# Retention and mixture of adapters, end of the program: two of six stores by Pool's queue, and one copy out of PSUM on ScalarE instead of VectorE

## The chip, the cores and the metric

The kernel runs on one core of a Trainium2 chip. The time is the device time of one execution in microseconds (us); the number that counts is the median over several runs. Beside it a profile of one further execution is there. Its span is the time from the first to the last instruction of the program on the core's engines, and the device time of that execution is a little longer than its span.

## The reference

Queries, keys and values have 8 batches, 8 heads, 576 positions and 64 columns, all in float32. First retention is computed: scaled scores, damped by a power of a constant of the head for each position of distance, nothing from the future, and then times the values. The heads are put side by side, which gives 4608 rows of 512. Each row then picks 2 of 8 adapters.

```
gamma = 1.0 - 2.0 ** (-5.0 - np.arange(H))
Dmat  = np.where(rel >= 0, gamma ** rel, 0.0)
attn  = np.matmul(scale * np.matmul(q, kT) * Dmat, v)
x     = attn.transpose(0, 2, 1, 3).reshape(B * S, H * D)
topk  = two largest of x @ w_gate, w = softmax over these two
out   = x + sum over the two: w * (x @ A[e]) @ B[e]
```

## The kernel before

The work is cut into units. A full unit is a chunk of 128 positions for two batches; a half unit is the last 64 positions (512 to 575) for four batches. For each four batches there are eight full units and one half unit, so `NU` is 18. The very last unit, `END`, is a half unit, and `END - 1` is the full unit before it. The order of the work is written out by hand: each engine does its instructions in the order in which the code emits them, and an instruction waits only for the data that it needs. A loop over the units keeps TensorE busy with the products of one unit while VectorE, ScalarE and Pool prepare operands for the next ones and copy results out of PSUM.

What matters here is what follows the loop, from L1028 on. The adapters of the last unit are chosen in two halves, n = 0 and n = 1, so that the second half can begin while the first is under way. After that the results leave PSUM in three steps:

- `osn_out(nc.vector, END - 1, n)`, for n = 0 and 1: VectorE copies half n of unit `END - 1` from the PSUM tile `po` to the SBUF tile `osb`, as 128 partitions by 512 values.
- `osh_out(END, 0, o, nc.scalar)`, for o = 0 and 1: ScalarE copies half 0 of unit `END`, in two pieces of 128 by 256, one for each of two PSUM banks.
- `osh_out(END, 1, o, nc.vector)`, for o = 0 and 1: VectorE copies half 1 of unit `END` in the same way. `Yn_mm` at L655 writes the two banks one after the other.

Then six stores are issued:

- `store(END - 1)` gives two stores (L702) of 128 rows of 2 KB, which is 256 KB each, one for each n. Both are issued by SyncE (SP in the profile).
- `store_rows(END, n, (nc.sync, nc.scalar))` gives, for each n, two stores (L717) of 64 rows of 2 KB, 128 KB each: `par` = 0 takes the lower 64 partitions and is issued by SyncE, `par` = 1 takes the upper 64 and is issued by ScalarE.

An engine that issues a store first waits until the copy has filled that part of `osb`. The stores of one engine are issued in the order of the code. At the end of the program (L1102) SyncE waits for all stores to land, after which the engines meet once more and the program is over. Pool (`nc.gpsimd`) issues two loads in the whole kernel before: `Wg` at L737 (16 KB) and `Bcat` at L903 (128 KB, with a conversion from float32 to float16). Pool's last computation is `q_turn` of the last unit, long before the end.

Of the kernel before, what the change touches and what calls it, by code (L numbers as in the profile page):

```python
# [21 lines left out]
def kernel(  # L22
# [10 lines left out]
    nc = tc.nc  # L33
# [91 lines left out]
    def full(u):  # L125
        return units[u][0] < NFULL
# [54 lines left out]
    def copy(eng, out, in_):  # L181
        if eng is nc.scalar:
            nc.scalar.copy(out=out, in_=in_)  # L183
        else:
            eng.tensor_copy(out=out, in_=in_)  # L185
# [489 lines left out]
    def osh_out(u, n, o, eng):  # L675

        s = st[u]
        copy(
            eng, s["osb"][:, n, :].rearrange("p (a o d) -> p o a d", a=HP, o=2)[:, o],
            s["pn"][n][o],  # L680
        )
# [6 lines left out]
            s["po"][:, :, n],  # L688
        )

    def store(u):
        c, bp = units[u]
        of = st[u]["osb"]
        tok = out.rearrange("(b s) d -> s b d", s=S)
        if full(u):


            parts = [(0, 0, 119), (1, 0, 128), (0, 119, 128)]
            if u > NU - 4:
                parts = [(0, 0, 128), (1, 0, 128)]  # L700
            for n, lo, hi in parts:
                nc.sync.dma_start(  # L702
                    out=tok[128 * c + lo : 128 * c + hi, 2 * bp + n, :], in_=of[lo:hi, n, :]
                )
            return
        for par in range(2):
            b = 4 * bp + 2 * par
            nc.sync.dma_start(
                out=tok[128 * c : 128 * c + 64, b : b + 2, :], in_=of[HALF[par]]
            )  # L710

    def store_rows(u, n, eng):

        c, bp = units[u]
        tok = out.rearrange("(b s) d -> b s d", s=S)
        for par in range(2):
            eng[par].dma_start(  # L717
                out=tok[4 * bp + 2 * par + n, 128 * c : 128 * c + 64, :],
                in_=st[u]["osb"][HALF[par], n, :],
            )  # L720
# [215 lines left out]
    osb_open(0)  # L936
    osb_out(nc.scalar, 0)
    store(0)
    route_s(1)
    U_out(2)  # L940
# [24 lines left out]
    END = NU - 1  # L965
    for r in range(2, END):
# [39 lines left out]
        osb_open(r - 1)  # L1006
        osb_out(nc.vector if nn < NU else nc.scalar, r - 1)
        store(r - 1)
        if nn < NU:
            T_open(nn, "q", "S")  # L1010
# [58 lines left out]
    for o in range(2):  # L1069
        osh_out(END, 0, o, nc.scalar)  # L1070
    for o in range(2):
        osh_out(END, 1, o, nc.vector)
    store(END - 1)
    for n in range(2):
        store_rows(END, n, (nc.sync, nc.scalar))
    return


# [28 lines left out]
```

## Time and profile before

| what | value |
|---|---|
| median of 3 runs | 180.52 us (180.03 to 184.05) |
| the profiled execution, device time | 180.89 us |
| the profiled execution, span | 179.1 us |
| mean granted TensorE clock | 0.991 of full speed |
| TensorE (PE) busy | 172.0 us, 96% of the span |
| VectorE (DVE) busy | 131.3 us, 73% |
| Pool busy | 121.9 us, 68% |
| ScalarE (ACT) busy | 77.5 us, 43% |

So the profiled execution lies 1.8 us above its own span, and 0.37 us above the median of the runs. In rows of the profile, PE, DVE, ACT, POOL and SP are the engines, and a name with a q behind it (SPq, ACTq) is that engine's instruction queue, where DMAs are issued and waited for. The DMA queues have numbers: q1 carries what SyncE issues, q10 what ScalarE issues, and q0, called software_dynamic, what Pool issues. Times of a timeline are us from the start of the span, start first, duration second.

### The profile page before, as it was taken

Reading aid. Unit: us, or ns where it says so; the run is one execution under the profiler, and the core shown is the slowest. Engines: PE = TensorE matmul, PEld = TensorE weight load, DVE = VectorE, ACT = ScalarE, POOL = GpSimd, SP = SyncE. Lnnn points to the kernel's source line nnn. Section 1 sums busy time; section 2 is a strip of 40 time slices with the busy share of each in tenths; the row PEclk is TensorE's granted clock in tenths of the full one; section 3 lists DMA queues with packets and bytes.
Section 4 is the critical chain, followed back from the end, with each engine's and each line's share of the span. In section 5 each row is a group of like instructions: output and inputs, shape, how many; then the busy total and the mean of one; then the engine's idle time right before and its main releaser. Section 6 shows DMA issues by size and latency. Waiting matters only on the chain.

```text
span 179.1 us, 9384 instructions
## 1 busy us (share of the span) xinstructions
PE 172.0 (96%) x4126; PEld 156.7 (87%) x4126; DVE 131.3 (73%) x236; ACT 77.5 (43%) x158; POOL 121.9 (68%) x208
## 2 busy tenths in 40 slices
PE   7999999999999999999999999999999999999990
PEld 5799988989999999989989999999998999889960
DVE  6586475789696968687676686969696869687870
ACT  0743644925252535352726362625252444443330
POOL 7990676497888688787994929585868677792000
PEclk9999999999999999999999999999999999999996
DMA  4999999989898989998999998999999999974125
GB/s 116 280 261 247 256 207 203 232 201 216 208 262 201 262 197 253 222 224 200 266 223 252 230 268 193 239 223 239 231 249 205 252 217 249 213 205 152 48 105 202
DMA packets 119368, 39.00 MB, mean 218 GB/s; under 512 B 114320, under 2 KB 114720, under 8 KB 119328
## 3 DMA queue, kind: packets, MB, share of 16 engines
q1 hardware_dynamic: 113360, 36.51, 84.1%
q10 hardware_dynamic: 5792, 1.75, 4.1%
q8 instruction: 32, 0.52, 1.1%
q0 software_dynamic: 176, 0.15, 0.5%
q14 instruction: 8, 0.07, 0.1%
HBM read 29.09 MB, written 9.44 MB: 215 GB/s over the span
## 4 chain that ended last, share of the span: by engine, by line
PE 95%; DVE 2%; issue 1%; DVEq 0%
PE pz L487 20%; PE px L432 18%; PE pu L395 9%; PE ps L322 9%; PE pt_k L248 6%; PE px L451 6%; PE po L620 5%; PE pt_q L248 5%; PE ps L304 4%; PE po L605 4%; PE pf L728 3%; PE pzt L587 2%; DVE M L373 2%; PE pa L514 1%; PE ps L338 1%
## 5 line engine op out<-in xcount | busy, mean ns | idle before, releaser
L373 DVE TENSOR_TENSOR M<-ps,tri 64x1024 f32<-64x1024 f32 (+1 forms) x34 | 37.3, 1097 | 4.8 <-PE ps L322 4.0
L185 POOL COPY M<-Qs 64x512 f32<-64x512 f32 x34 | 20.8, 612 | 26.1 <-ACT Qs L183 25.3
L487 PE MATMUL pz<-AW,xT 128*128 128x136 f32 x288 | 37.7, 284 | 0.0
L432 PE MATMUL px<-M,W 128*64 128x128 f32 (+1 forms) x640 | 35.4, 263 | 0.4 <-DVE M L373 0.4
L487 PEld LDWEIGHTS pz<-AW,xT 128*128 128x128 f32 x288 | 34.6, 190 | 0.6
L226 POOL TENSOR_TENSOR k<-k,pack 128x1024 f32<-128x1024 f32 (+1 forms) x18 | 32.5, 1808 | 2.4 <-POOL V L185 0.8
L185 POOL COPY W<-v 64x256 f32<-64x256 f32 x78 | 28.9, 396 | 7.5 <-DMA v<-in_v_dram 5.8
L183 ACT COPY kT<-pt_k 128x1024 f32<-128x1024 f32 x17 | 17.3, 1016 | 37.6 <-PE pt_k L248 37.6
L432 PEld LDWEIGHTS px<-M,W 128*64 128x64 f32 x640 | 31.8, 137 | 0.8 <-POOL k L226 0.6
L470 DVE TENSOR_TENSOR xT<-px,gx 128x1024 f32<-128x1024 f32 x11 | 13.5, 1225 | 15.7 <-PE px L451 14.1
L185 DVE COPY osb<-po 128x1024 f32<-128x1024 f32 (+2 forms) x18 | 19.2, 1074 | 6.0 <-PE po L620 5.3
L596 ACT COPY zT<-pzt 128x256 f16<-128x256 f16 (+1 forms) x19 | 6.9, 362 | 36.6 <-PE pzt L587 36.6
L183 ACT COPY M<-pt_q 64x512 f32<-64x512 f32 x35 | 20.2, 577 | 1.1 <-PE pt_q L248 0.6
L395 PE MATMUL pu<-v,k 128*64 128x64 f32 x512 | 18.4, 225 | 0.0
L322 PE MATMUL ps<-Qs,kT 64*64 64x128 f32 (+1 forms) x304 | 18.2, 260 | 0.0
L322 PE MATMUL ps<-M,kT 64*64 64x128 f32 (+1 forms) x304 | 18.0, 259 | 0.0
L188 POOL TENSOR_TENSOR W<-pn,W 64x512 f32<-64x512 f32 x12 | 15.3, 1273 | 3.7 <-ACT pn L183 2.9
L395 PEld LDWEIGHTS pu<-v,k 128*64 128x64 f32 x512 | 16.2, 138 | 1.1
L322 PEld LDWEIGHTS ps<-M,kT 64*64 64x64 f32 x304 | 14.9, 134 | 0.2
L322 PEld LDWEIGHTS ps<-Qs,kT 64*64 64x64 f32 x304 | 14.9, 134 | 0.0
L248 PEld LDWEIGHTS pt_k<-ident,k 64*128 64x128 f32 x272 | 9.9, 139 | 3.2 <-issue 2.9
L185 POOL COPY V<-v 64x256 f32<-64x256 f32 x32 | 12.0, 401 | 0.7
(75 smaller groups left out, 298.8 us busy)
## 6 DMA issues: line engine op xcount, KB each, us to landing
v<-in_v_dram SPq DMA_DIRECT2D x36, 256.0 KB
q<-in_q_dram SPq DMA_DIRECT2D x35, 256.0 KB
k<-in_k_dram SPq DMA_DIRECT2D x33, 256.0 KB
out_dram<-osb SPq DMA_DIRECT2D x20, 256.0 KB
out_dram<-osb SPq DMA_DIRECT2D x14, 238.0 KB
k<-in_k_dram ACTq DMA_DIRECT2D x3, 256.0 KB
An<-in_moe_A_dram ACTq DMA_DIRECT2D x1, 256.0 KB
q<-in_q_dram ACTq DMA_DIRECT2D x1, 256.0 KB
```

Of the source, the lines that this page charges most:

```text
L183: nc.scalar.copy(out=out, in_=in_)
L185: eng.tensor_copy(out=out, in_=in_)
L188: eng.tensor_tensor(out=out, in0=a, in1=b, op=ALU.add)
L226: eng.tensor_tensor(out=kt, in0=kt, in1=gv[:, c, :].unsqueeze(1).unsqueeze(3).broadcast_to((128, bs.stop - bs.start, H, Dh)), op=ALU.mult,)
L248: mm(ps[:, r, hp, b, :], lhsT=src[HALF[r], b * H + 2 * hp : b * H + 2 * hp + 2, :], rhs=ident[HALF[r], 64 * r : 64 * r + 64], is_transpose ...
L322: mm(s["ps0"][HALF[1 - p], b, hp, sl], lhsT=s["kT"][HALF[ho], x, hp, b, :], rhs=Q_of(u, b, ho, hp, sl), start=(hp == 0 and x == 0), stop=True,
L373: nc.vector.tensor_tensor(out=s["M"][sl, p, bs].rearrange("p b a i -> p (b a) i"), in0=s["ps0"][sl, bs].rearrange("p b a i -> p (b a) i"), ...
L395: mm(s["pu"][HALF[p], b, hp, :], lhsT=nat[("k", u)][:, h, :], rhs=nat[("v", u)][:, h, :], start=(hp == 0 and b == 0), stop=True, skip_grou ...
L432: mm(s["pxb"][b][HALF[ho], hp, sl], lhsT=s["W"][x][:, p, b, hp, :], rhs=s["M"][:, p, b, hp, sl], start=(hp == 0 and x == 0), stop=True, sk ...
L451: mm(s["px"][HALF[ho], b, hp, HI], lhsT=vv, rhs=s["S1"][HALF[p], b, hp, :], start=False, stop=True, skip_group_check=True,)
L470: nc.vector.tensor_tensor(out=s["xT"][:, bs].rearrange("p b a i -> p b (a i)"), in0=s["px"][:, bs].rearrange("p b a i -> p b (a i)"), in1= ...
L487: mm(s["pz"][:, n, :], lhsT=s["xT"][:, n, dt, :], rhs=AW[:, dt, :], start=(dt == 0), stop=(dt == HP - 1), skip_group_check=True,)
```

## The change

Three edits, all in the last lines of the program. The store of half 1 of unit `END - 1` (256 KB) and the store of half 0, `par` = 1, of unit `END` (128 KB) are issued by Pool's queue, in this order; before, the first was SyncE's and the second was ScalarE's. Of the two copies of half 1 of unit `END`, the one of o = 1 goes from VectorE to ScalarE, behind ScalarE's two copies of half 0.

```
-    def store(u):
+    def store(u, eng=None):
...
-                nc.sync.dma_start(
+                (eng[n] if eng else nc.sync).dma_start(
...
-        osh_out(END, 1, o, nc.vector)
-    store(END - 1)
+        osh_out(END, 1, o, (nc.vector, nc.scalar)[o])
+    store(END - 1, (nc.sync, nc.gpsimd))
     for n in range(2):
-        store_rows(END, n, (nc.sync, nc.scalar))
+        store_rows(END, n, (nc.sync, (nc.gpsimd, nc.scalar)[n]))
```

The other calls of `store` pass no engine and so stay with SyncE.

## The prediction

> **What bounds the kernel now.** I read the page first, then the chain that ended last, then only the last 6 us: the timeline engine by engine, the DMA's share by stretches, and SyncE's waits. The page has the whole and the chain has its tail:
>
> ```profile
> span 179.1 us, 9384 instructions
> PE 172.0 (96%) x4126; PEld 156.7 (87%) x4126; DVE 131.3 (73%) x236; ACT 77.5 (43%) x158; POOL 121.9 (68%) x208
> ```
> ```profile
> 173.89 0.23 PE po L655
> 174.12 0.03 issue
> 174.15 0.42 DVE osb L185
> 174.57 0.33 DVEq L1102
> ```
>
> TensorE bounds the kernel up to 174.12 us, and no edit touches anything before that: copies and stores of the last two units are downstream of the last products. What the change can move is the 5 us from there to the end. In them the copies come first (the first row is the second half of `END - 1`; ScalarE's two copies are half 0 of `END`, VectorE's last two are half 1):
>
> ```profile
> 173.29 0.68 DVE L185 COPY osb<-po 128x512 f32<-128x512 f32 x1
> 173.54 0.65 ACT L183 COPY osb<-po 128x256 f32<-128x256 f32 x2
> 173.83 0.39 PE L655 MATMUL po<-Bcat,zT 128*128 128x256 f16 x2
> 174.15 0.42 DVE L185 COPY osb<-po 128x256 f32<-128x256 f32 x1 [0.18 <-PE po L655]
> 174.49 0.41 DVE L185 COPY osb<-po 128x256 f32<-128x256 f32 x1
> ```
>
> then the six stores, two of 256 KB (L702) and four of 128 KB (L717):
>
> ```profile
> 173.40 0.33 SPq L702 DMA_DIRECT2D out_dram<-osb  x1
> 174.00 0.33 SPq L702 DMA_DIRECT2D out_dram<-osb  x1
> 174.22 0.54 ACTq L717 DMA_DIRECT2D out_dram<-osb  x1
> 174.42 0.53 SPq L717 DMA_DIRECT2D out_dram<-osb  x1
> 174.93 0.47 ACTq L717 DMA_DIRECT2D out_dram<-osb  x1
> 175.04 0.63 SPq L717 DMA_DIRECT2D out_dram<-osb  x1
> ```
>
> and then only transfers. The columns that matter in the stretches below are the last two, DMA share and GB/s:
>
> ```profile
> 173.50:174.00 0.50, 0.50 (x11) 0.37 (x10) 0.47 (x1) 0.50 (x3) 0.00 (x0) 1.00 0.00 0
> 174.00:174.50 0.50, 0.22 (x2) 0.00 (x0) 0.35 (x2) 0.19 (x1) 0.00 (x0) 1.00 0.52 205
> 174.50:175.00 0.50, 0.00 (x0) 0.00 (x0) 0.40 (x2) 0.00 (x0) 0.00 (x0) 1.00 1.06 406
> 175.75:176.00 0.25, 0.00 (x0) 0.00 (x0) 0.00 (x0) 0.00 (x0) 0.00 (x0) 0.79 0.98 197
> 177.25:177.50 0.25, 0.00 (x0) 0.00 (x0) 0.00 (x0) 0.00 (x0) 0.00 (x0) 0.50 0.32 107
> 177.50:179.10 1.60, 0.00 (x0) 0.00 (x0) 0.00 (x0) 0.00 (x0) 0.00 (x0) 0.50 0.00 1
> ```
>
> The DMA engines start about 174.25 and are practically through at 177.5. Six stores are 2 x 256 + 4 x 128 = 1024 KB, 1.05 MB; at the 406 GB/s of a full stretch they need 2.6 us, and they take 3.25. So the end is nearly bound by transfer, with about 0.65 us of slack in it. Last comes SyncE's wait at L1102; two looks at it, between 177.6 and 178.04 and after that:
>
> ```profile
> L1102 SPq EVENT_SEMAPHORE  x1: 28/28/28, 178.0 to 178.0; - x1
> L1102 SPq EVENT_SEMAPHORE  x5: 17/28/28, 178.1 to 179.0; - x5
> SPq L1102 <- DMA out_dram<-osb: 2.2, 3, 1.3
> ```
>
> The last landing is therefore at 178.0, about 0.5 us after the last bytes, and 1.1 us of shutdown follow whatever happened before. The span changes as the last landing does.
>
> **The change, part by part.** (a) The copy. VectorE's second piece ends now at 174.49 + 0.41 = 174.90. ScalarE is through with its own two at 173.54 + 0.65 = 174.19, TensorE with the second bank at 173.83 + 0.39 = 174.22; ScalarE's third copy of the same shape then runs from about 174.27 for 0.37:
>
> ```profile
> L183 ACT COPY osb<-po x4: 373/694/1014, 31.5 to 173.8; 128x1024 f32<-128x1024 f32 x2, 128x256 f32<-128x256 f32 x2
> ```
>
> and ends at 174.64, with VectorE's first piece at 174.57. Half 1 is ready 0.26 us earlier. This holds only because ScalarE's store of half 0 goes away: it occupied ScalarE's queue from 174.22 to 174.76, and a copy behind it would have ended after 175.1.
>
> (b) The four stores that stay with SyncE and ScalarE. SyncE's list loses the store at 174.00; its store of half 0 needs ScalarE's copies (174.19), so it goes out about 174.25 in place of 174.42, and the last one after 0.53 plus the same gap of 0.09 (174.95 to 175.04), at 174.87 in place of 175.04: 0.17 us earlier. ScalarE's last goes out at 174.67 in place of 174.93, 0.26 earlier. From issue to the end of SyncE's wait the last store took 178.0 - 175.04 = 2.96. Part of that was queueing behind stores that are now elsewhere. ScalarE's last bounds it from below: the wait before the final one ended about 177.4 (the same view, between 177.2 and 177.6, below), 2.47 after 174.93.
>
> ```profile
> L1102 SPq EVENT_SEMAPHORE  x1: 28/28/28, 177.4 to 177.4; - x1
> ```
>
> So these four land last at 174.87 + 2.47 to 2.96 = 177.34 to 177.83: a gain of 0.17 to 0.66.
>
> (c) Pool's two stores. Pool has been idle since 163.68 (its last copies, first row below), so nothing is queued behind them, and they cost no engine time that anybody waits for. The only Pool DMAs of this trace are the loads `Bcat` and `Wg`, and no store of Pool is in it. `Bcat` has the form of the first store, 128 rows; `Wg` is cut into 512 small pieces:
>
> ```profile
> 162.41 1.27 POOL L185 COPY M<-Qs 64x512 f32<-64x512 f32 x2 [1.39 <-ACT Qs L183]
> 23.08 0.59 POOL L903 DMA_DIRECT2D Bcat<-in_moe_B_dram  x1
> 23.72 0.39 POOL L185 COPY W<-v 64x256 f32<-64x256 f32 x1
> DMA to landing us min/median/max: 3.9/3.9/3.9
> L737 POOL DMA_DIRECT2D Wg<-in_moe_w_gate_dram x1: 948/948/948, 1.3 to 1.3; - x1
> DMA to landing us min/median/max: 4.7/4.7/4.7
> ```
>
> Pool's first store waits for VectorE's copy (173.29 + 0.68 = 173.97) and goes out about 174.05, as SyncE did at 174.00. The second needs ScalarE's copies (174.19, past by then) and follows 0.64 later, as Pool's next instruction followed `Bcat` (23.08 to 23.72): 174.69. With the issue time of `Wg` it would be 174.05 + 0.95 + 0.05 = 175.05.
>
> When does the second one land? Three prices. *By landing rows, whole:* 174.69 + 3.9 = 178.59 with `Bcat`, 0.59 later than 178.0; 175.05 + 4.7 = 179.75 with `Wg`, 1.75 later. *By its pieces:* in the DMA view, no packet of q0 moves from 23.08 to 25.14, and between 25.14 and 26.65 all of `Bcat`'s packets do, beside traffic of q1:
>
> ```profile
> q1 hardware_dynamic: 848, 0.21, 64.0%
> q0 software_dynamic: 144, 0.13, 53.0%
> ```
>
> So Pool's first byte moves 2.06 us after the issue, SyncE's first one 174.25 - 173.40 = 0.85 after. The first store's data start at 174.05 + 2.06 = 176.11. If Pool's 384 KB then had the engines to themselves at 406 GB/s, they would take 0.97 us, to 177.08, and with 0.5 from the last bytes to the landing 177.58, 0.42 *earlier* than 178.0; then the hardware queues' 177.34 to 177.83 decide. *With sharing:* SyncE's and ScalarE's last two stores (256 KB) go out at 174.67 and 174.87, at nearly the same place of the transfer as Pool's; the issue at 174.22 of ScalarE moved no data before 175.5, 1.3 later, so these two start about 176.0. Then 640 KB (655 thousand bytes) run from 176.05 at 406 GB/s for 1.61 us, to 177.66, landing 178.16: 0.16 *later* than now. The saving of (a) and (b) is paid back, because DMA engines that were full from 174.5 to 175.5 stand nearly idle while Pool's descriptors are prepared.
>
> ```profile
> DMA  9999499599599490959999090990990099974963
> q10 hardware_dynamic: 69, 0.13, 85.5%
> q1 hardware_dynamic: 31, 0.03, 12.7%
> ```
>
> One more term has two signs. This is the DMA view from 175.50 to 176.19: engines shown busy, but only 0.16 MB moved (197 GB/s in the stretch above), while ScalarE's store of half 0 ran. At full rate this is 0.4 us of work in 0.69 us. The trace doesn't say why; if Pool's store is spared it, 0.29 us is gained, and if it befalls a longer stretch, as much is lost. I leave it at zero in the middle and in the range on both sides.
>
> Between the shared pieces (+0.16) and `Bcat` whole (+0.59, which contains the crowded 1.5 us of its packets) I take the middle, **+0.35 us**: rows nearest in form, sharing of about the same degree.
>
> The Trainium skill, "DMA: Bandwidth & Descriptors", section "Anatomy of one DMA — SWDGE (gpsimd) path", gives a Pool DMA a fixed 2.0 us and then 436 KB per us; 2.3 us for 128 KB, an estimate from that page. The trace does not agree: `Bcat`, of this size, took 3.9. By that rule Pool's second store would land at 174.69 + 2.3 = 177.0, before the hardware queues' last, and the sum would be the gain of (b), rival 1 below.
>
> **Sum.** 180.89 (the profiled execution) + 0.35 = 181.24. That execution lies 0.37 above the median of the runs, so in terms of the median: 180.52 + 0.35 = **180.9 us**.
>
> **The rivals.** *1. Pool is in time.* Its data start at 176.11 and run unhindered; SyncE's last store ends the program, 0.17 to 0.66 earlier, mean 0.4: 180.1. For it: 0.65 us of slack in the transfer, which three queues may fill better than two. Against it: the 3.9 and the 4.7. Chance 0.28. *2. Pool's preparation is long.* If the first store after 10 idle us goes as `Wg` did, 0.95 to issue and 4.7 to land, the program ends 1.75 later: 182.3; halfway, 181.6. It decides once Pool's second store lands after 178.6. For it: `Wg` too was issued when Pool had hardly worked before. Against: its 512 pieces have no counterpart here. Chance 0.20. *3. One after the other.* If Pool's second store is prepared only when the first has landed, it lands at 174.05 + 3.9 + 3.9 = 181.85, 3.85 later: 184.4. Against: Pool went on to a copy 0.64 after `Bcat`. Chance 0.03. *4. The edit does nothing for half 1*, because ScalarE's third copy is held up: only by 174.90 would the gain of (a) be gone, and since SyncE's last store goes out at 174.87 anyway, that costs under 0.1. Chance 0.02, 180.9 too.
>
> **How the numbers follow.** The forecast, 180.5 to 181.3, has 0.47. The range goes from rival 1's better half (180.52 - 0.6 = 179.9) to rival 2's bound (182.3). A measurement of this kernel can tell about 2%, 3.6 us, from no change. No row lets a gain reach that: even no transfer time at all past 174.9 would save 178.0 - 174.9 = 3.1 us. Rival 3 alone exceeds it on the other side. Hence 0.01 faster, 0.95 within, 0.04 slower.
>
> **What would show it.** Copies of half 1 ending at 174.6 in place of 174.9; SyncE's last issue at about 174.9; two Pool issues of about 0.6 us from 174.05 on; q0's first store packet at about 176.1, with a stretch of low DMA share before it, around 175 to 176; and Pool's second store the last to land, at 178.2 to 178.6. It is wrong if SyncE's or ScalarE's store lands last (rival 1), if q0 starts after 177 (rival 2), or if the two Pool stores don't overlap (rival 3).

## The result, and the profile after

| | before | after |
|---|---|---|
| median | 180.78 us (180.03 to 184.05, 8 runs) | 181.83 us (181.14 to 182.67, 8 runs) |
| ratio to before | | 1.0071, 95% interval 1.0045 to 1.0097 |
| profiled execution, device time and span | 180.89, 179.1 us | 182.67, 180.9 us |
| end of the last matmul (L655) | 174.22 us | 175.33 us |
| from there to the end of the span, "the tail" | 4.87 us | 5.56 us |

The change makes the kernel slower by less than 2%. The profiled execution after is the slowest of its eight, and it must be split before it is read: 1.1 us of the longer span lie before the last matmul, where the two programs are the same, and 0.69 us after it. Over all the kernels of this study, which are the same up to that matmul, it ended anywhere between 173.38 and 175.49 us (176.31 in e4), so the first part is read as scatter between executions. The tail belongs to the change: profiled twice, it was 5.56 and 5.55 us. All times below are therefore counted from the end of the last matmul, written +1.24, unless they stand in a profile row; second digits of spans and landings are from the trace's records. Executions over 1.5% above the fastest of their kernel, such as the 184.05 in the table and the one that e4's profile is of (182.90), count in no ratio, so e4 is judged by its ratio first.

The timeline after, engine by engine (start, duration). First the copies, then the six issues:

```profile
173.81 1.28 DVE L185 COPY osb<-po 128x512 f32<-128x512 f32 x2
174.66 1.08 ACT L183 COPY osb<-po 128x256 f32<-128x256 f32 x3
174.94 0.39 PE L655 MATMUL po<-Bcat,zT 128*128 128x256 f16 x2
175.26 0.42 DVE L185 COPY osb<-po 128x256 f32<-128x256 f32 x1 [0.17 <-PE po L655]
```
```profile
174.52 0.33 SPq L702 DMA_DIRECT2D out_dram<-osb  x1
175.33 0.53 SPq L717 DMA_DIRECT2D out_dram<-osb  x1
175.39 0.60 POOL L702 DMA_DIRECT2D out_dram<-osb  x1 [10.60 <-DVE osb L185]
175.77 0.54 ACTq L717 DMA_DIRECT2D out_dram<-osb  x1
175.96 0.54 SPq L717 DMA_DIRECT2D out_dram<-osb  x1
175.99 0.54 POOL L717 DMA_DIRECT2D out_dram<-osb  x1
```

The copies did what was foreseen. Half 1 is ready at 174.66 + 1.08 = 175.74, which is +0.41, against +0.68 before (174.90 - 174.22). The last issues of SyncE and ScalarE moved with it: +0.63 and +0.44, against +0.82 and +0.71.

Next, the stretches after the last matmul, before and after, cut at the same distances (0, 0.5, 0.75, 1.25, 1.75 us, for the kernel after on to 2.75). The last two columns are the DMA engines' share and GB/s:

```profile
174.22:174.72 0.50, 0.00 (x0) 0.00 (x0) 0.50 (x2) 0.00 (x0) 0.00 (x0) 1.00 0.94 369
174.72:174.97 0.25, 0.00 (x0) 0.00 (x0) 0.18 (x1) 0.00 (x0) 0.00 (x0) 1.00 1.08 410
174.97:175.47 0.50, 0.00 (x0) 0.00 (x0) 0.00 (x0) 0.00 (x0) 0.00 (x0) 1.00 1.09 422
175.47:175.97 0.50, 0.00 (x0) 0.00 (x0) 0.00 (x0) 0.00 (x0) 0.00 (x0) 0.93 1.04 250
```
```profile
175.33:175.83 0.50, 0.00 (x1) 0.00 (x0) 0.36 (x1) 0.37 (x1) 0.44 (x1) 1.00 0.94 369
175.83:176.08 0.25, 0.00 (x0) 0.00 (x0) 0.00 (x0) 0.00 (x0) 0.25 (x2) 1.00 0.82 311
176.08:176.58 0.50, 0.00 (x0) 0.00 (x0) 0.00 (x0) 0.00 (x0) 0.45 (x1) 1.00 0.05 16
176.58:177.08 0.50, 0.00 (x0) 0.00 (x0) 0.00 (x0) 0.00 (x0) 0.00 (x0) 1.00 0.85 250
177.08:177.58 0.50, 0.00 (x0) 0.00 (x0) 0.00 (x0) 0.00 (x0) 0.00 (x0) 1.00 1.03 311
177.58:178.08 0.50, 0.00 (x0) 0.00 (x0) 0.00 (x0) 0.00 (x0) 0.00 (x0) 0.89 0.93 307
```

This is the place of the loss. Before, the engines are full from 0 to +1.25. After, they move SyncE's first store and then stand nearly idle for half a microsecond (16 GB/s). By +1.25 the kernel before has moved 0.5 x 369 + 0.25 x 410 + 0.5 x 422 = 498 KB (thousands of bytes), the kernel after 184 + 78 + 8 = 270. The 228 KB that are missing are 0.57 us of work at 400 GB/s, and the last landing is later by about as much: SyncE's final wait ends at 179.7 (179.69, +4.36), before at 178.0 (+3.78). That the two agree is no proof; e2, e3 and e8 together price the store directly, below.

```profile
L1102 SPq EVENT_SEMAPHORE  x1: 28/28/28, 178.9 to 178.9; - x1
L1102 SPq EVENT_SEMAPHORE  x1: 28/28/28, 179.7 to 179.7; - x1
L1102 SPq EVENT_SEMAPHORE  x7: 17/28/28, 179.8 to 180.8; - x7
L702 POOL DMA_DIRECT2D out_dram<-osb x1: 604/604/604, 175.4 to 175.4; - x1
DMA to landing us min/median/max: 3.1/3.1/3.1
L717 POOL DMA_DIRECT2D out_dram<-osb x1: 541/541/541, 176.0 to 176.0; - x1
DMA to landing us min/median/max: 3.4/3.4/3.4
```

Pool's second store lands 3.4 after its issue, at +4.08; what lands last is SyncE's store of half 1, at +4.34. The shutdown behind the last landing has grown by 0.12, too. SyncE goes through a fixed list of waits, and those that stand behind the store that lands last still have to be gone through, about 0.06 us each: seven follow here, five before (the `x5` in the prediction's view). Pool's two stores bring two semaphores, which make the list one wait longer. The rest is a matter of place, for e10, which has no store on Pool, has seven too, and 1.20 us from the last landing to the end against 1.10 before:

```profile
L1101 SPq EVENT_SEMAPHORE  x7: 17/28/28, 179.5 to 180.6; - x7
```

The 0.58 and the 0.12 are, but for rounding, the 0.69 of the tail.

### The profile page after: what moved, and what is told of

It is laid out like the page before. It is cut to its first block, busy times and chain, and to the rows that moved or that the text cites. A ratio compares the mean times of both kernels' runs of the same rounds, so it can differ in the third digit from the quotient of the medians.

```text
span 180.9 us, 9384 instructions
## 1 busy us (share of the span) xinstructions
PE 172.6 (95%) x4126; PEld 157.1 (87%) x4126; DVE 131.0 (72%) x235; ACT 78.0 (43%) x159; POOL 123.1 (68%) x210
## 4 chain that ended last, share of the span: by engine, by line
PE 93%; DVE 2%; issue 1%; POOL 0%; POOLq 0%; DVEq 0%
PE pz L487 19%; PE px L432 17%; PE pu L395 9%; PE ps L322 9%; PE pt_k L248 6%; PE px L451 6%; PE po L620 5%; PE pt_q L248 5%; PE po L605 4%; PE ps L304 4%; PE pf L728 3%; PE pzt L587 2%; DVE M L373 2%; PE pa L514 1%; PE ps L338 1%
```

## The experiments

Each quoted text below was written before its run. Theory A, as most of them call it, was that the large store on Pool costs: its data come late, the engines stand idle, everything after shares what is left. The rivals were that the copies count in full, that two Pool stores stand in each other's way, or that any store of Pool is late. All times and ratios first; each tail is of one profiled execution. The edits of e1, e2, e8 and e10 are shown against the change, those of e5 and e6 against the kernel before:

| kernel | tail, us | ratio, 95% interval |
|---|---|---|
| before | 4.87 | |
| the change | 5.56 | 1.0071 (1.0045 to 1.0097) |
| e1 stores on Pool, copies as before | 6.09 | 1.0085 (1.0051 to 1.0119) |
| e2 copy edit alone | 4.93 | 0.9987 (0.9957 to 1.0017) |
| e3 the change, only the 256 KB store on Pool | 5.47 | 1.0022 (0.9992 to 1.0052) |
| e4 the change, only the 128 KB store on Pool | 4.81 | 0.9980 (0.9945 to 1.0016) |
| e5 before, but the first 256 KB store on Pool | 5.41 | 1.0041 (1.0008 to 1.0075) |
| e6, e7 half 0 and half 1 in one store each, without and with the copy edit | 14.56, 14.40 | 1.0545 (1.0507 to 1.0583), 1.0562 (1.0530 to 1.0593) |
| e8 no 256 KB store of half 1 at all | 4.86 | |
| e9 the change again | 5.55 | 1.0037 (0.9999 to 1.0074) |
| e10 two stores of 64 partitions, both halves each | 5.46 | 1.0023 (0.9974 to 1.0072) |
| e11 both stores of half 0 on Pool | 5.93 | 1.0073 (1.0027 to 1.0118) |
| e12 only the last store on Pool | 5.15 | 1.0018 (0.9990 to 1.0045) |

**e1, the stores without the copy edit.**

```
-        osh_out(END, 1, o, (nc.vector, nc.scalar)[o])
+        osh_out(END, 1, o, nc.vector)
```

> The change with its copy edit undone: VectorE copies both pieces of half 1 again, the two stores stay with Pool. Measure: from the end of the last matmul (L655) to the end of the span, 4.87 us before and 5.55 us after the change. Theory A (the tail is bound by transfer: Pool's large store moves no data for over 1 us, the DMA engines stand idle, and everything lands together later): the copy edit buys almost nothing, this part is 5.5 to 5.75 us. Rival B (the copies count in full, the last store goes out 0.2 us later): 5.75 to 5.9 us. On the time before the last matmul, 174.2 before and 175.3 after: if it is scatter between executions, it falls anywhere from 173.5 to 175.5 here; if Pool's stores change it, near 175.3.

6.09, above both. The copy edit inside the change is worth 0.53 us, twice the 0.27 by which it makes half 1 ready earlier. Without it the last stores of SyncE and ScalarE go out at +0.71 and +0.72, and their data run side by side from 2.6 to 4.3, at first beside Pool's second store as well (the DMA view from +2.81 to +4.31):

```profile
q10 hardware_dynamic: 77, 0.12, 24.5%
q0 software_dynamic: 38, 0.09, 23.9%
q1 hardware_dynamic: 76, 0.12, 21.6%
```

Each takes 1.5 us, where in the change they take 0.58 and 0.95 one after the other. Why they run so is not settled.

**e2, the copy edit alone.**

```
-    store(END - 1, (nc.sync, nc.gpsimd))
+    store(END - 1)
...
-        store_rows(END, n, (nc.sync, (nc.gpsimd, nc.scalar)[n]))
+        store_rows(END, n, (nc.sync, nc.scalar))
```

> The copy edit alone: all six stores as before, so ScalarE's store of half 0 goes out only behind its third copy, about 0.45 us later than before, and its store of half 1 another 0.55 after that. Theory A: the transfer has a slack of 0.65 us, so the tail from the last matmul is 4.9 to 5.2 us (before 4.87). Rival B (the copies count in full): SyncE's last store is 0.17 earlier, 4.7 us. Time against before: A 1.000 to 1.002, B 0.999.

4.93 and a ratio whose interval holds 1: no effect that these runs can tell, as A had it, though one step of it was wrong. ScalarE's store of half 0 did not wait behind the third copy:

```profile
174.32 0.82 ACT L183 COPY osb<-po 128x256 f32<-128x256 f32 x2
174.83 1.22 ACTq L717 DMA_DIRECT2D out_dram<-osb  x2
```

The third copy runs from +0.04 to +0.41 (174.77 to 175.14) and the store is issued at 174.83, while it runs: it needs the first two copies only. So the copy edit needed no Pool store to make room for it, and on its own it buys nothing.

**e3 and e4, one store on Pool each.**

```
e3: store(END - 1, (nc.sync, nc.gpsimd)); store_rows(END, n, (nc.sync, nc.scalar))
e4: store(END - 1); store_rows(END, n, (nc.sync, (nc.gpsimd, nc.scalar)[n]))
```

> The change with only the 256 KB store of unit END-1 on Pool; the 128 KB store of half 0 is ScalarE's again, behind the third copy. Theory A (late data of the large store leave the engines idle and then share them): the tail from the last matmul stays at 5.3 to 5.6 us, with a stretch of about 0.5 us of low DMA share after SyncE's first store. Rival B (the loss comes of two Pool stores one behind the other, the second landing late): 4.8 to 5.0 us.

> The change with only the 128 KB store of half 0 on Pool; both 256 KB stores of unit END-1 are SyncE's again. Theory A: no idle stretch, since SyncE's two large stores keep the engines busy for 1.3 us while Pool prepares; the tail from the last matmul is 4.7 to 5.0 us (before 4.87, after 5.55). Rival B (any store of Pool lands late or slows the others' packets): 5.3 to 5.6 us.

5.47 and 4.81: both as theory A said. The large store alone brings nearly the whole loss in the tail (its ratio, 1.0022, is too near 1 to tell by itself), and the hole in the transfer with it (e3, from +0.75 to +1.25, then the next half microsecond):

```profile
174.14:174.64 0.50, 0.00 (x0) 0.00 (x0) 0.00 (x0) 0.00 (x0) 0.00 (x0) 1.00 0.12 41
174.64:175.14 0.50, 0.00 (x0) 0.00 (x0) 0.00 (x0) 0.00 (x0) 0.00 (x0) 1.00 0.81 233
```

The small one alone, behind 1.4 us of SyncE's data, shows no cost: the ratio is 0.9980.

**e5, the other large store on Pool.** It is to tell the hole from the mixing of Pool's packets with others.

```
-    store(END - 1)
+    store(END - 1, (nc.gpsimd, nc.sync))
```

> The kernel before with one edit: of the two 256 KB stores of unit END-1, Pool issues the first (half 0, ready 0.7 us earlier) and SyncE the second. Everything else as before. It tells the idle stretch from the mixing of Pool's packets with the others. Theory A1 (the idle stretch is what costs: 1.2 us from Pool's issue to its first data): Pool's data start about 0.45 us after the end of the last matmul and SyncE's about 0.65, no hole later, and the tail from the last matmul is 4.9 to 5.2 us (before 4.87, large store of half 1 on Pool 5.47). Rival A2 (mixed packets run at 230 to 335 GB/s in place of 400, whenever they run): 512 KB mixed at 280 GB/s take 1.9 us, then the small ones; tail 5.3 to 5.7 us.

The tail, 5.41, is in A2's range, but A2's mechanism falls. While Pool's and SyncE's large stores run together, from +0.80 on, the engines move 410 GB/s (third row, +1.0 to +1.5):

```profile
173.76:174.26 0.50, 0.00 (x0) 0.00 (x0) 0.50 (x2) 0.00 (x0) 0.06 (x1) 1.00 0.00 0
174.26:174.76 0.50, 0.00 (x0) 0.00 (x0) 0.18 (x1) 0.00 (x0) 0.00 (x0) 1.00 0.76 311
174.76:175.26 0.50, 0.00 (x0) 0.00 (x0) 0.00 (x0) 0.00 (x0) 0.00 (x0) 0.77 1.01 410
```

What is wrong is the start. Data begin at +0.65 in place of +0.02, and the last landing is 0.48 later (+4.25), the tail 0.54 longer. A1 had a late start right, if too early (0.45), and the price wrong: most of the lateness at the front goes through to the end.

**e8, without the large store.**

```
-    store(END - 1, (nc.sync, nc.gpsimd))
+    store(END - 1, ns=(0,))
...
-        store_rows(END, n, (nc.sync, (nc.gpsimd, nc.scalar)[n]))
+        store_rows(END, n, (nc.sync, nc.scalar))
```

`store` passes over a half that is not in `ns`, so these 128 rows of the output are not written.

> The change with the 128 KB store of half 0 back on ScalarE, and the 256 KB store of half 1 of unit END-1 left out (its 128 rows of the output are not written). It is the run with only the large store on Pool (tail 5.47 us, last landing 4.32 after the last matmul) less that store. Theory A2 (Pool's packets slow the four small stores): the last landing is at 3.2 to 3.5, and the packets of 2 KB take 84 ns. Rival (the small stores are slow in themselves, whatever runs beside them): data of the small stores still begin 1.4 us after their issue, packets of 150 ns, last landing 3.6 to 4.0.

The last landing is at +3.69 and the tail 4.86 (one execution), as before with that store: the rival. A quarter of all bytes is gone and nothing is won. The prediction held the end of the kernel before to be nearly bound by the engines' rate; by this run it is not.

With e2 and e3 this also prices the store itself, since the three have the same copies and differ only in who issues it. Nobody (e8): last landing +3.69, tail 4.86. SyncE (e2): +3.83, 4.93. Pool (e3): +4.32, 5.47. Issued by SyncE the store is nearly free, for its data move from +0.67 to +1.45, when the engines have hardly anything else to move: SyncE's first store ends at about +0.8, and the first small store's data begin only at 1.2 to 1.4. Issued by Pool its data begin at +1.24, nearly together with those of the small stores, and the first of these takes 1.45 us in e3, 0.80 in e8.

The packets show what the end does wait for. Below, each queue's packets are cut, in their order, by the number of packets of each store; the columns are start of issue, first data, end of data and last landing, in us from the last matmul:

```
                              issue   data           landed
before  SyncE   256 KB        -0.82   0.02 to 0.76   1.24
        SyncE   256 KB        -0.22   0.68 to 1.47   1.83
        ScalarE 128 KB         0.00   1.31 to 2.06   2.44
        SyncE   128 KB         0.20   1.89 to 2.39   2.79
        ScalarE 128 KB         0.72   2.22 to 2.81   3.17
        SyncE   128 KB         0.83   2.54 to 3.42   3.77
after   SyncE   256 KB        -0.81   0.03 to 0.81   1.16
        SyncE   128 KB        -0.00   1.40 to 2.76   3.33
        Pool    256 KB         0.06   1.24 to 2.68   3.14
        ScalarE 128 KB         0.44   2.51 to 3.09   3.52
        SyncE   128 KB         0.63   3.05 to 4.00   4.34
        Pool    128 KB         0.66   2.88 to 3.68   4.08
e3      SyncE   256 KB        -0.82   0.02 to 0.81   1.15
        SyncE   128 KB        -0.00   1.39 to 2.84   3.38
        Pool    256 KB         0.05   1.24 to 2.75   3.19
        ScalarE 128 KB         0.10   2.50 to 3.09   3.56
        SyncE   128 KB         0.63   2.83 to 3.75   4.15
        ScalarE 128 KB         0.74   3.05 to 3.83   4.32
e8      SyncE   256 KB        -0.81   0.03 to 0.82   1.16
        SyncE   128 KB        -0.01   1.18 to 1.98   2.34
        ScalarE 128 KB         0.10   1.77 to 2.31   2.67
        SyncE   128 KB         0.63   2.09 to 2.63   3.00
        ScalarE 128 KB         0.73   2.42 to 3.32   3.69
```

In before, after and e8 SyncE's and ScalarE's stores stand in one line over both queues: their data begin in the order of issue, each as the one before it comes to its end (they overlap by up to 0.3 us). The order of first data is the same in every kernel of this study, but the line is no strict rule: in e1 the last two overlap by 1.4 us, in e3 by 0.7 and in e5 by 0.6, the latter two when Pool's data had ended. A small one takes 0.5 to 0.9 us in this line without Pool, as much as a large one of twice the bytes (0.74 to 0.79), and the first of them runs slowly (packets of 2 KB in 150 ns, in the others 84 in the median). In the kernel before this line has no gap. In e8 it has one, from 0.82 to 1.18, because a small store's first data come 1.2 us after its issue, and that and the long last store (0.90) eat what the missing store leaves.

**e6 and e7, one store of 128 rows for each half.**

```
-    for n in range(2):
-        store_rows(END, n, (nc.sync, nc.scalar))
+    tokb = out.rearrange("(b s) d -> b s d", s=S)
+    for n in range(2):
+        b0 = 4 * units[END][1] + n
+        (nc.sync, nc.scalar)[n].dma_start(
+            out=tokb[b0 : b0 + 3 : 2, S - 64 : S, :], in_=se["osb"][:, n, :]
+        )
```

> The kernel before with the four 128 KB stores made into two of 256 KB: each half of unit END goes out as one store of 128 rows (two pieces of 64 rows in memory), half 0 by SyncE and half 1 by ScalarE; copies as before, no Pool. Theory A (the engines' rate and holes set the tail, and stores of 64 rows cost 0.53 us to issue and 1.3 to 1.45 us to their first data where those of 128 rows cost 0.33 and 0.85): data run without a break at 400 GB/s from 0 to 2.65 us after the last matmul, the last landing is at 3.0 to 3.2 in place of 3.78, tail 4.1 to 4.4 us, ratio 0.996 to 0.998. Rival B (the slow stretch belongs to memory and not to the form of the store): tail 4.7 to 4.9 us, ratio 0.999 to 1.001.

> The same two merged stores and the copy edit of the change (half 1 copied by VectorE and ScalarE). Theory A: half 1 goes out 0.28 us earlier, but the engines are busy with half 0 until then, so the tail is that of the merged stores alone within 0.15 us, 4.1 to 4.4 us. Rival B (the last issue sets the end): 0.25 us less than without the copy edit.

Both missed by 10 us. The share of the DMA engines that work is 0.13, which is two of sixteen (e6):

```profile
174.00:174.50 0.50, 0.00 (x0) 0.00 (x0) 0.26 (x1) 0.00 (x0) 0.00 (x0) 1.00 1.07 410
176.00:178.00 2.00, 0.00 (x0) 0.00 (x0) 0.00 (x0) 0.00 (x0) 0.00 (x0) 1.00 0.13 32
182.00:184.00 2.00, 0.00 (x0) 0.00 (x0) 0.00 (x0) 0.00 (x0) 0.00 (x0) 0.50 0.13 51
```

The outermost dimension of the destination is the two batches. The Trainium skill, "DMA: Bandwidth & Descriptors", section "Why a DMA increments its semaphore by 16 and not by 1", says that a DMA is spread over the largest number of engines, at most 16, that divides the outermost sizes of both of its sides; here that is 2, and the trace agrees with 0.13. The question that the two runs were for, whether fewer stores help, they leave open.

**e9, the change again.**

> The change itself once more, for a second profile and a narrower time. If what it costs lies after the last matmul alone (5.56 us against 4.87), the ratio is 1.003 to 1.005 and the tail again 5.4 to 5.7 us, with the end of the last matmul anywhere between 173 and 176 us. If the change also costs time before that, the ratio is 1.007 or more and the last matmul ends after 175 again.

The tail is the same to 0.01 us; the ratio agrees with the tail alone, 0.69 / 180.5 = 0.38%, though its interval (0.9999 to 1.0074) also reaches from no change to the 0.71% of the first comparison. The last matmul ended at 175.49, late as in the first profile and as the other reading had it. But the kernel before took longer in these runs too (median 181.62), and in e1 and e3, with the same large store on Pool, that matmul ended at 173.38 and 173.39. The interval of the first comparison begins just above 0.38%. What is left over between the two is not explained by any trace here.

**e10, two stores of 64 partitions.**

```
-    for n in range(2):
-        store_rows(END, n, (nc.sync, (nc.gpsimd, nc.scalar)[n]))
+    store(END, (nc.sync, nc.scalar))
```

with `store(END - 1)` on SyncE; for a half unit `store` now takes the engine of each of its two stores from `eng`.

> The copy edit of the change, no store on Pool, and the four 128 KB stores made into two of 256 KB in another way: 64 partitions with both halves of unit END each, the lower by SyncE, the upper by ScalarE, both once half 1 is copied (0.41 us after the last matmul). Theory A (few stores, data without long breaks): issue at 0.45, first data at 1.8, 512 KB at 400 GB/s to 3.1, last landing 3.4 to 3.6, tail 4.5 to 4.7 us (before 4.87). Rival B (stores of 64 partitions move at 200 GB/s until the issue is far behind): last landing 3.9 to 4.6, tail 5.0 to 5.7.

Rival B, 5.46. Both stores are issued together; two stretches of the DMA view follow, 1.72 to 3.03 and 3.07 to 3.97 after the last matmul:

```profile
175.66 0.64 SPq L708 DMA_DIRECT2D out_dram<-osb  x1
175.67 0.70 ACTq L708 DMA_DIRECT2D out_dram<-osb  x1
```
```profile
DMA packets 125, 0.26 MB, mean 195 GB/s; under 512 B 0, under 2 KB 0, under 8 KB 125
q1 hardware_dynamic: 125, 0.26, 94.9%
```
```profile
DMA packets 153, 0.26 MB, mean 287 GB/s; under 512 B 27, under 2 KB 27, under 8 KB 153
q10 hardware_dynamic: 141, 0.26, 79.1%
```

In the first only q1 moves, in the second q10 moves the whole of its store: the one line again, at its plainest. And the first store of 64 partitions runs at 195 GB/s.

**e11 and e12, looking for a version that gains.**

```
e11: store(END - 1); store_rows(END, n, ((nc.gpsimd, nc.gpsimd), (nc.sync, nc.scalar))[n])
e12: store(END - 1); store_rows(END, n, (nc.sync, (nc.scalar, nc.gpsimd)[n]))
```

> The copy edit, both 256 KB stores of unit END-1 on SyncE, both 128 KB stores of half 0 on Pool, those of half 1 on SyncE and ScalarE. Theory A (Pool's late first data cost nothing while SyncE's large stores fill the engines): Pool's issues at 0.26 and 0.85, SyncE's and ScalarE's last issues at 0.45, last landing 3.4 to 3.7 us after the last matmul, tail 4.55 to 4.85 (before 4.87). Rival B (two Pool stores are late in themselves): the second lands after 4.0, tail over 5.1.

> The copy edit; both 256 KB stores and both lower 128 KB stores on SyncE, the upper one of half 0 on ScalarE, and only the last, the upper one of half 1, on Pool. Theory L (SyncE's and ScalarE's stores move their data in one line, one after the other in the order of issue, and the end is the length of this line): the line loses its last-but-one store of 0.5 to 0.6 us, while Pool's data (issue at about 0.7, first data at 1.9) run beside it; last landing 3.3 to 3.6 us after the last matmul against 3.78 before, tail 4.4 to 4.7, ratio 0.996 to 0.999. Rival M (a store of Pool beside small stores costs the line as much as it takes out of it): last landing 3.7 to 4.2, tail 4.8 to 5.3, ratio 1.000 to 1.003.

Neither gains. e11 lands last at +4.64, ScalarE's store; Pool's second at +4.39, with SyncE's, ScalarE's and Pool's small stores together at only 150 to 250 GB/s. e12 lands at +3.99: taking a store out of the line shortened it by a place, but SyncE's last store, beside Pool's, then began at 2.69 and ended at 3.61, later than before. Rivals B and M, in size and in place. No version of this study beats the kernel before by more than its interval; e4 comes nearest, 0.9980 (0.9945 to 1.0016).

## Why the prediction was right, and where not

**The size and the sign.** Within 2%, a little slower, was forecast, and it came so: the tail grew by 0.69, for a forecast of +0.35. (The ratio of the first comparison, 0.71%, is more than the tail; see e9.) The sum was too small by half, from two terms. The landing was 0.58 later, in place of 0.35 (and the top of the working, `Bcat` whole, was 0.59); and 0.12 came from the shutdown, which was taken to be fixed whatever happened before it. That step failed: what follows the last landing depends on how many waits stand behind it, as e10 shows without any store on Pool.

**The path.** The forecast let Pool's second store land last, at 178.2 to 178.6 (+3.98 to +4.38), and named a store of SyncE or ScalarE landing last as a sign of being wrong. That sign came. Pool's second store did land where it was foreseen, at +4.08, but SyncE's last store landed after it, at +4.34, where the working had +3.12 to +3.61 (177.34 to 177.83). So the sign and half of the size came out right while another store than the one in the working ended the program. That the middle of two prices was near is partly luck.

**(a) the copy.** Right: 0.27 earlier for 0.26. Wrong in its condition: e2 shows that ScalarE issues its store while the third copy runs.

**(b) the issues.** Right in size: 0.19 (+0.82 to +0.63) and 0.27 earlier, for 0.17 and 0.26. What should follow from them, a landing 0.17 to 0.66 earlier, failed, and this is the term that was furthest off. SyncE's last store was issued at +0.63, its data began at +3.05, behind ScalarE's, and it landed 0.57 later than before. The delay from issue to landing is no property of the store, as the term had it; it grew from 2.96 to 3.7.

**(c) Pool's stores.** The first was issued 0.23 us later than foreseen: VectorE's copy ends at 173.81 + 1.28 = 175.09, Pool issues at 175.39, where SyncE took 0.03. Its first data came 1.18 us after the issue (+0.06 to +1.24), not the 2.06 of `Bcat`; the first issue took 0.60 and the second followed 0.60 after the first, for 0.59 and 0.64. The errors run against each other: Pool's data began 0.65 earlier than the forecast's +1.89, and still it was late.

**The hole.** This was the right step, in the right place: idle engines around 175 to 176 while Pool prepares (in the profile after, 176.08 to 176.58). The sum by sharing at 406 GB/s gave 0.16, because it took 406 GB/s for what then moves at 250 to 311 (from 176.58 to 178.08, with small stores in the line). The term of two signs, the slow first small store, was left at zero. It did not go away: its 2 KB packets take 147 to 153 ns in before, e2, e8 and e10, which have no store on Pool, and still 109 in the median in the change. The 0.65 us of slack in the transfer were no slack, as e8 shows: with a quarter less to move the end came at the same time.

**The rule for a Pool DMA.** By the Trainium skill, "DMA: Bandwidth & Descriptors", section "Anatomy of one DMA — SWDGE (gpsimd) path", an estimate for a store of Pool is 2.3 us for 128 KB and 2.6 for 256 KB; the first of these stands beside rival 1. Measured from issue to landing, the first store on Pool took 2.3 for 128 KB in e11 and 2.6 for 256 KB in e5, as the rule has it, but 2.5 and 2.9 for 128 KB in e4 and e12, and 3.1 for 256 KB in the change. A second one, 128 KB, took 3.4 in the change, 3.6 in e11 and 3.7 in e1. The rule comes near for a store that moves early; beside and behind small stores it is short by up to 1.4 us.

**The rivals.** 1 fell, as SyncE's store does land last but later, not earlier, than before. 2 and 3 fell, as Pool's preparation was shorter than either load's and its two stores overlap in time. 4 fell, as the third copy was not held up: half 1 was ready at +0.41.

## What to carry to other kernels

When stores end a program, look at when each one's first and last data move, not only at the issues. Here a store was nearly free while its data moved before the next stores' data could begin (e2 against e8), and cost 0.5 us where a queue with a later start brought its data among theirs (e3), even though the engine that issued it was idle. Give such a queue a small store that others' data cover for that time (e4), or none. And making data ready earlier was worth nothing where the stores stood in a line (e2), though 0.53 us beside two stores on Pool (e1 against the change).

## What the runs showed of the hardware that was not expected

- The data of stores issued by SyncE and by ScalarE began in the order of issue over both queues in every kernel here, and mostly each as the one before it came to its end; in e10 two issued together went almost wholly one after the other. The Trainium skill, "DMA: Bandwidth & Descriptors", section "Rules for kernel authors", says that two transfers of disjoint partition halves serialize, since both use the same engines, with the packets of two queues interleaved. In e10 they do serialize, but one whole after the other, hardly interleaved; in e1 the two halves run side by side.
- The first store of 64 partitions had its first data 1.2 to 1.4 us after the issue (128 partitions: 0.84), and without a store on Pool its packets of 2 KB took about 150 ns (195 GB/s in e10), those of most later ones 84. Why is open.
- Pool's stores go in packets of 4 KB: q0 has 128 packets more than before for 384 KB, 96 of data and two times 16 for semaphores.

```profile
q0 software_dynamic: 304, 0.54, 1.1%
```
